# Denominators divided in token layout, sixteen-tile query sets, and gated loads in a fused linear attention and PReLU MLP

## The chip, the cores and the metric

One Trainium2 chip, one of its cores. The metric is the device time of one execution in microseconds (us); several executions of each kernel are taken and their median is used. Engines: TensorE (PE; its weight loads are PEld), VectorE (DVE), ScalarE (ACT), GpSimd (POOL), SyncE (SP), which issues most DMAs.

## The reference

q, k, v are 4 batches x 4 heads x 1088 tokens x 32, in float32. S1 and S2 are 8 x 32.

```python
def phi(x):                       # 64 features of a token
    a, b = S1 @ x, S2 @ x         # 8 and 8
    return outer(a, b).reshape(64)
kv  = sum_s phi(k)[f] * v[d]      # per batch and head, 64 x 32
z   = sum_s phi(k)                # 64
x   = (phi(q) @ kv) / (phi(q) @ z + 1e-6)     # 32 per head; four heads give 128
h   = x @ w_in                    # 4352 x 128 times 128 x 2048
g   = max(h, 0) + alpha * min(h, 0)
out = g @ w_out                   # 2048 x 128
```

## The kernel before, in words

Since g = (1 - alpha) * max(h, 0) + alpha * h, the MLP is a relu between two matmuls, plus one matmul with W = w_in diag(alpha) w_out, made once. `w_out_bf` holds w_out scaled by 1 - alpha, `w_b_f` holds w_out scaled by alpha; `winT` is w_in transposed (L319, L322); W is made at L330.

All work is written as operations (`Op`) with an engine or a choice of engines, an estimated duration, a priority and the buffers that they take and free. `schedule` lists them greedily: at each step it takes the operation that can start first, within 60 ns the one with the lowest priority number, and so fixes the order on every engine. The order is fixed when the program is built; the engines run it in order and wait for each other by semaphores. `PRIO` holds the priority bases, `UNITS` the query units, `GROUPS` the MLP's column groups. PSUM has eight banks: A0 to A3 (used by queries and keys), H0 to H2 (the first matmul's output, keys too), O (the second matmul's accumulator).

- `keys(b)`: k of a batch is transposed in blocks of 32 (VectorE, L344), multiplied by S1 and S2 (L352), transposed back to token layout (L359), and a times b gives `phi` (VectorE or POOL, L372). L404 sums phi times v over tokens on TensorE. The sum z comes for batches 0 and 1 from the same kind of products with ones, for 2 and 3 from additions of phi (L387 to L393) and one product with ones (L425). L436 transposes the result into `kz`.
- `queries(u)`: a unit of up to 1024 tokens. `qT` (L459), then features with S1 and S2 spread to 64 rows: the A part (L465) is copied out of PSUM to `a_sb` (L474), the B part (L465 again) is multiplied with it into `qp` (L480). L492 multiplies by the z part of `kz`, then by its kv part. The denominators go back to token layout (L503), are inverted (L508, L509), transposed forward again (L514) and multiplied onto the numerators (L517) into `xT`. All four A banks are held as one set through these passes.
- `mlp(g)`: for a group of columns of `xT`, 16 times: a matmul into an H bank (L533), a relu out of it to `rh` by ScalarE (L540) or VectorE (L542), a matmul into O (L546); then the one with W (L553). O is transposed to `oT` on VectorE (L558) and stored by SP.

Loads are issued by SP in the order of a list, without waits: rows (S1, S2, alpha), k0, part of q0, v0, the weights, then k, q, v of batch 1, of 2, of 3.

Of the kernel before, what the change touches and what calls it, by code (L numbers as in the profile page):

```python
# [18 lines left out]
UNITS = ((0, 256), (512, 288), (1088, 512), (2112, 512), (3136, 512), (4160, 96))  # L19
GROUPS = ((0, 512), (512, 288), (800, 288), (1088, 512), (1600, 512), (2112, 512), (2624, 512), (3136, 512),  # L20
          (3648, 512), (4160, 192))

Z_PE = (True, True, False, False)

PRIO = {"W": 5147, "w": 18782, "k": [-27032, -767, -3337, 2408], "q": [-6698, -3807, 1309, 2997, 24174, 8836]}
# [17 lines left out]
class Op:  # L43
    def __init__(self, eng, fn, prio, deps=(), takes=(), frees=(), lat=150, after=0):
# [3 lines left out]
        self.takes, self.lat, self.after = list(takes), lat, after  # L48
        for h in frees:
            h.frees.append(self)  # L50
        self.end = None


def schedule(ops, slots):


    free_at = {}
# [18 lines left out]
    while ready:  # L76
        best = None
        for o in ready:
            t0 = max([d.end + d.lat for d in o.deps] + [o.after])
# [3 lines left out]
            for h in o.takes:  # L83
                cand = sorted((slot_free(s), s) for s in h.names if s not in taken and slot_free(s) is not None)
# [19 lines left out]
        t, _, end, o, e, dur, picks = min(near, key=lambda b: (b[1], b[2]))  # L104
        o.end, free_at[e] = end, end
        for h, names in zip(o.takes, picks):
            h.got = names
            for s in names:
                holder[s] = h
# [6 lines left out]
    assert len(order) == len(ops), "operations left"  # L116
# [4 lines left out]
def kernel(  # L121
# [32 lines left out]
    rows = sb("rows", [2 * r + NC, 128])  # L154
    q_sb = sb("q_sb", [128, T])
    qT = sb("qT", [128, T])
# [6 lines left out]
    w_b_f = sb("w_b_f", [128, NC, DM])  # L163
# [4 lines left out]
    ones = sb("ones", [128, 32])  # L168
    ST = sb("ST", [128, 2 * r + NC])
    mask2 = sb("mask2", [128, 2])  # L170
    Sk = sb("Sk", [128, 2, 2 * r])
    Sa = sb("Sa", [128, r, r])
    Sb = sb("Sb", [128, r, r])
    oma = sb("oma", [128, NC])
    kz = [sb(f"kz{b}", [128, 2, 128]) for b in range(B)]

    A = psum.tile([128, 4, 512], F32, tag="A", name="A")
    bank = {f"A{i}": A[:, i] for i in range(4)}
    for i in range(3):
        bank[f"H{i}"] = psum.tile([128, 512], F32, tag=f"H{i}", name=f"H{i}")  # L180
    bank["O"] = psum.tile([128, 512], F32, tag="O", name="O")
# [13 lines left out]
    P_ab = pool("ab", 2, [128, 2, KW * 32])  # L195
    P_phi = pool("phi", 2, [128, 2, KW, 2, R])
    P_ps = pool("phs", 1, [128, 4, 2, 2, R])
    P_kv = pool("kvs", 2, [128, 2, 2, R])
    P_as = pool("a_sb", 1, [128, H, 512])
    P_qp = pool("qp", 1, [128, H, 512])  # L200
    P_dt = pool("dt", 1, [128, 2, 16, 32])
    P_rc = pool("rc", 2, [128, 2, 16])
    P_rr = pool("rr", 1, [128, 2, 512])
# [10 lines left out]
    def act(n):  # L214
        return (172 + n) / 1.2 - 10

    def dve(n):
        return (120 + n) / 0.96
# [11 lines left out]
    loads = []  # L230

    def load(name, kb, fn, after=()):
        loads.append((name, kb, fn))

    def l_rows():
        for i, x in enumerate((S1, S2)):
            dma("sync", rows[i * r:(i + 1) * r].rearrange("p (h d) -> p h d", h=H),
                dram(x, 0, [[D, r], [0, H], [1, D]]))
        dma("sync", rows[2 * r:], dram(moe_alpha, 0, [[128, NC], [1, 128]]))

    def l_k(b):
        dma("sync", k_sb[b], dram(k, b * H * S * D, [[S, 128], [1, S]]))

    def l_v(b):
        for g in range(4):
            dma("sync", v_sb[b][32 * g:32 * (g + 1)].rearrange("p h w d -> p h (w d)"),
                dram(v, b * H * S * D + K0[g] * D, [[NB * D, 32], [S * D, H], [1, KW * D]]))
# [8 lines left out]
    def l_wout(i):  # L256
        dma("sync", w_out_f[:, 8 * i:8 * (i + 1)],
            dram(moe_w_out, 8 * i * 128 * DM, [[DM, 128], [DM * 128, 8], [1, DM]]))

    plan = [("rows", 24, l_rows), ("k0", 557, lambda: l_k(0)), ("q0a", 262, lambda: l_q(0, 0, 16)),  # L260
            ("v0", 557, lambda: l_v(0)), ("wo0", 524, lambda: l_wout(0)), ("wi0", 524, lambda: l_win(0)),
            ("wi1", 524, lambda: l_win(1)), ("wo1", 524, lambda: l_wout(1)),
            ("k1", 557, lambda: l_k(1)), ("q0b", 295, lambda: l_q(0, 16, NB)), ("v1", 557, lambda: l_v(1)),
            ("q1", 557, lambda: l_q(1, 0, NB)), ("k2", 557, lambda: l_k(2)), ("v2", 557, lambda: l_v(2)),
            ("q2", 557, lambda: l_q(2, 0, NB)), ("k3", 557, lambda: l_k(3)), ("v3", 557, lambda: l_v(3)),
            ("q3", 557, lambda: l_q(3, 0, NB))]
    L = {}
    t = 700.0
    for i, (name, kb, fn) in enumerate(plan):
        t += max(kb / 0.30, 1200 if name == "rows" else 300)  # L270
        L[name] = op(("SP", 1), fn, -1000 + i, after=0, lat=0)
        L[name].lat = t + 1800


    c_ident = op(("POOL", 700), lambda: make_identity(nc, ident), -900)

    def f_masks():
        nc.vector.memset(ones, 1.0)
        nc.vector.memset(mask2, 0.0)
        for h in range(H):  # L280
            nc.vector.memset(mask2[h * D:(h + 1) * D, h % 2:h % 2 + 1], 1.0)
    c_mask = op(("DVE", 600), f_masks, -900)
    h_rows = Hold(HBANKS)
    c_rt = op(("PE", 300), lambda: nc.tensor.transpose(
        bank[h_rows.got[0]][:, :2 * r + NC], rows, ident[:2 * r + NC, :2 * r + NC]),
        -890, deps=[L["rows"], c_ident], takes=[h_rows], lat=250)
    c_st = op(("DVE", 200), lambda: nc.vector.tensor_copy(ST, bank[h_rows.got[0]][:, :2 * r + NC]),
# [3 lines left out]
    c_sa = op(("ACT", 250), lambda: nc.scalar.copy(Sa, view(ST, [[1, r], [0, r]])), -870, deps=[c_st])  # L291
    c_sb = op(("ACT", 250), lambda: nc.scalar.copy(Sb, view(ST, [[0, r], [1, r]], r)), -870, deps=[c_st])
    c_om = op(("DVE", 150), lambda: nc.vector.tensor_scalar(
        oma, ST[:, 2 * r:], -1.0, 1.0, op0=mybir.AluOpType.mult, op1=mybir.AluOpType.add), -800, deps=[c_st])


    c_win, c_wo, c_wb, c_wT = [], [], [], []
    for i in range(4):
        c_win.append(op(("ACT", 610), lambda i=i: nc.scalar.copy(
            w_in_bf[:, 512 * i:512 * (i + 1)], w_in_f[:, 512 * i:512 * (i + 1)]), PRIO["w"] + i, deps=[L[f"wi{i // 2}"]]))  # L300
    for i in range(4):
        s = slice(4 * i, 4 * i + 4)

        def scaled(e, dst, al, s=s):
            if e == "POOL":
                nc.gpsimd.tensor_mul(dst[:, s], w_out_f[:, s], view(al[:, s], [[1, 4], [0, 128]]))
            else:
                for c in range(s.start, s.stop):
                    nc.scalar.mul(dst[:, c], w_out_f[:, c], al[:, c:c + 1])
# [307 lines left out]
```

## Time and profile before

| | |
|---|---|
| median of 3 runs (lowest to highest) | 135.97 us (135.4 to 136.08) |
| profiled execution, its own time | 135.97 us |
| its span, first to last instruction | 134.2 us |
| mean granted TensorE clock | 0.983 |
| busy share of PE, DVE, ACT, POOL | 82%, 72%, 53%, 18% |
| DMA | 11.37 MB, 24271 packets |

A line of a group reads: source line, engine, operation, output and inputs with their shapes, count, then busy us, mean ns of one, and the idle time of that engine just before, with what ended it. TensorE's matmuls overlap and their ends are modelled, so its busy share overstates it; a float32 product counts as two instructions.

### The profile page before, as it was taken

Reading aid. Unit: us, or ns where it says so; the run is one execution under the profiler, and the core shown is the slowest. Engines: PE = TensorE matmul, PEld = TensorE weight load, DVE = VectorE, ACT = ScalarE, POOL = GpSimd, SP = SyncE. Lnnn points to the kernel's source line nnn. Section 1 sums busy time; section 2 is a strip of 40 time slices with the busy share of each in tenths; the row PEclk is TensorE's granted clock in tenths of the full one; section 3 lists DMA queues with packets and bytes.
Section 4 is the critical chain, followed back from the end, with each engine's and each line's share of the span. In section 5 each row is a group of like instructions: output and inputs, shape, how many; then the busy total and the mean of one; then the engine's idle time right before and its main releaser. Section 6 shows DMA issues by size and latency. Waiting matters only on the chain.

```text
span 134.2 us, 3241 instructions
## 1 busy us (share of the span) xinstructions
PE 110.1 (82%) x1315; PEld 54.4 (41%) x1315; DVE 96.4 (72%) x177; ACT 71.0 (53%) x152; POOL 24.6 (18%) x28
## 2 busy tenths in 40 slices
PE   0053899899499995988979799799998999999970
PEld 0011589565365442522724233243442444434540
DVE  0179527869999985998947775697768778598450
ACT  3105965050106944665365764497936858468640
POOL 2009740451770000992000000000000000000000
PEclk9999999999958999999999999999999999999998
DMA  1999999998000005003030001400500405014041
GB/s 31 299 255 374 358 238 334 272 286 204 26 5 7 0 3 77 0 0 49 0 48 1 0 0 24 60 0 0 78 0 12 71 0 78 0 22 68 11 67 29
DMA packets 24271, 11.37 MB, mean 85 GB/s; under 512 B 18736, under 2 KB 22848, under 8 KB 24256
## 3 DMA queue, kind: packets, MB, share of 16 engines
q1 hardware_dynamic: 24256, 11.16, 35.1%
q8 instruction: 10, 0.16, 0.6%
q14 instruction: 5, 0.04, 0.1%
HBM read 8.93 MB, written 2.23 MB: 83 GB/s over the span
## 4 chain that ended last, share of the span: by engine, by line
PE 67%; DVE 20%; DMA 4%; ACT 3%; issue 2%; SPq 1%; DVEq 0%; ACTq 0%
PE O L546 20%; PE H L533 20%; PE A L492 7%; PE A L465 6%; DVE phi L372 6%; PE H L404 5%; DVE a_sb L474 4%; DVE dt L503 4%; DMA k_sb<-in_k_dram 4%; ACT a_sb L474 3%; DVE qp L480 2%; PE H L330 2%; PE A L352 2%; DVE ab L359 2%; PE H L319 1%
## 5 line engine op out<-in xcount | busy, mean ns | idle before, releaser
L540 ACT ACTIVATE rh<-H 128x512 bf16<-128x512 f32 (+2 forms) x115 | 55.5, 532 | 26.4 <-PE H L533 24.2
L533 PE MATMUL H<-xT,w_in_bf 128*128 128x512 bf16 (+2 forms) x160 | 46.6, 348 | 1.2 <-DVE rh L542 0.6
L546 PE MATMUL O<-rh,w_out_bf 128*128 128x512 bf16 (+2 forms) x160 | 42.5, 347 | 0.0
L542 DVE TENSOR_SCALAR rh<-H 128x512 bf16<-128x512 f32 (+2 forms) x45 | 27.4, 612 | 5.8 <-PE H L533 4.8
L533 PEld LDWEIGHTS <-w_in_bf 128*128 128x128 bf16 x160 | 14.4, 97 | 22.0 <-issue 10.5
L546 PEld LDWEIGHTS <-w_out_bf 128*128 128x128 bf16 x160 | 15.5, 97 | 16.1 <-issue 2.7
L372 POOL TENSOR_TENSOR phi<-ab 128x512 f32<-128x512 f32 (+1 forms) x9 | 11.8, 1334 | 33.7 <-DVE ab L359 26.7
L492 PE MATMUL A<-qp,kz 64*32 64x512 f32 (+7 forms) x224 | 10.5, 439 | 3.3 <-DVE dt L503 2.8
L474 ACT COPY a_sb<-A 128x1024 f32<-128x1024 f32 (+2 forms) x5 | 4.3, 852 | 16.1 <-PE A L465 16.1
L480 DVE TENSOR_TENSOR qp<-a_sb,A 128x1024 f32<-128x1024 f32 (+3 forms) x12 | 10.4, 901 | 2.9 <-PE A L465 2.9
L404 PE MATMUL H<-phi,v_sb 128*32 128x64 f32 (+1 forms) x288 | 11.0, 268 | 1.2 <-issue 1.1
L558 DVE STREAM_TRANSPOSE oT<-O 128x512 f32<-128x512 f32 (+2 forms) x10 | 6.3, 628 | 5.8 <-PE O L553 5.0
L404 PEld LDWEIGHTS H<-phi,v_sb 128*32 128x32 f32 (+1 forms) x288 | 7.6, 137 | 5.6 <-issue 5.1
L474 DVE COPY a_sb<-A 128x1024 f32<-128x1024 f32 (+3 forms) x7 | 5.7, 829 | 5.7 <-ACT a_sb L474 5.7
L372 DVE TENSOR_TENSOR phi<-ab 128x640 f32<-128x640 f32 (+1 forms) x7 | 9.7, 1413 | 0.0
L465 PE MATMUL A<-qT,Sb 32*64 32x512 f32 (+3 forms) x96 | 5.7, 531 | 4.5 <-DVE a_sb L474 4.5
L503 DVE STREAM_TRANSPOSE dt<-A 128x512 f32<-128x512 f32 (+3 forms) x12 | 6.0, 538 | 2.8 <-PE A L492 2.8
L344 DVE STREAM_TRANSPOSE kT<-k_sb 128x544 f32<-128x544 f32 x8 | 5.6, 717 | 2.6 <-DMA k_sb<-in_k_dram 2.6
L352 PE MATMUL A<-kT,Sk 64*32 64x288 f32 x32 | 2.6, 549 | 5.4 <-DVE kT L344 4.0
L465 PE MATMUL A<-qT,Sa 32*64 32x512 f32 (+3 forms) x96 | 5.7, 530 | 1.1 <-DVE ab L359 1.1
L404 PE MATMUL H<-phi,ones 128*32 128x64 f32 (+1 forms) x144 | 6.4, 267 | 0.0
L514 DVE STREAM_TRANSPOSE rr<-rc 128x512 f32<-128x512 f32 (+3 forms) x12 | 5.9, 534 | 0.2
(65 smaller groups left out, 85.7 us busy)
## 6 DMA issues: line engine op xcount, KB each, us to landing
v_sb<-in_v_dram SPq DMA_DIRECT2D x16, 144.0 KB, 8.1
k_sb<-in_k_dram SPq DMA_DIRECT2D x4, 544.0 KB, 9.8
q_sb<-in_q_dram SPq DMA_DIRECT2D x3, 544.0 KB, 8.7
out_dram<-oT SPq DMA_DIRECT2D x20, 64.0 KB, 2.0
w_out_f<-in_moe_w_out_dram SPq DMA_DIRECT2D x2, 512.0 KB, 8.4
w_in_f<-in_moe_w_in_dram SPq DMA_DIRECT2D x2, 512.0 KB, 7.8
q_sb<-in_q_dram SPq DMA_DIRECT2D x1, 288.0 KB, 8.8
out_dram<-oT SPq DMA_DIRECT2D x8, 36.0 KB, 3.0
```

The costliest lines, as they stand in the source:

```text
L372: eng.tensor_mul(bufs[hph.got[0]][:, rr_, w0:w0 + m // 2].rearrange("p w h f -> p (w h) f"), view(src, [[16, m], [1, r], [0, r]], o0), vie ...
L404: nc.tensor.matmul(kb[32 * h:32 * (h + 1), (R if z else 0):(R if z else 0) + R], ones[rows_] if z else v_sb[b][rows_, h, w], p[rows_, rr_, ...
L465: nc.tensor.matmul(A[64 * c:64 * (c + 1), h, :n], S_[32 * h:32 * (h + 1)].rearrange("p i j -> p (i j)"), qT[32 * h:32 * (h + 1), col0 + c ...
L474: ca[-1].fn = lambda e, i=i: copy(e)(bufs[has.got[0]][:, 2 * i:2 * i + 2, :n], A[:, 2 * i:2 * i + 2, :n])
L480: mu.append(op(("DVE", dve(2 * n)), lambda i=i: nc.vector.tensor_mul(bufs[hqp.got[0]][:, 2 * i:2 * i + 2, :n], bufs[has.got[0]][:, 2 * i:2 ...
L492: nc.tensor.matmul(A[32 * h:32 * (h + 1), 2 * o + c, x0 - lo:x1 - lo], kz[b][64 * c:64 * (c + 1), o, 32 * h:32 * (h + 1)], bufs[hqp.got[0] ...
L503: nc.vector.transpose(bufs[hdt.got[0]][:, c, :nb].rearrange("p a b -> p (a b)"), A[:, 2 + c, :n])
L533: hm = op(("PE", n / 2.4 + 3), lambda c=c, hh=hh: nc.tensor.matmul(bank[hh.got[0]][:, :n], w_in_bf[:, c * 128:(c + 1) * 128], xT[:, col0:c ...
L540: nc.scalar.activation(bufs[hr.got[0]][:, :n], bank[hh.got[0]][:, :n], ACTF.Relu)
L542: nc.vector.tensor_scalar_max(bufs[hr.got[0]][:, :n], bank[hh.got[0]][:, :n], 0.0)
L546: nc.tensor.matmul(bank["O"][:, :n], w_out_bf[:, c], bufs[hr.got[0]][:, :n], start=state["n"] == 0, stop=state["n"] == last)
L558: ev = op(("DVE", dve(n)), lambda: nc.vector.transpose(bufs[ho.got[0]][:, :nb].rearrange("p a b -> p (a b)"), bank["O"][:, :n]), prio - 5, ...
```

## The change

Keys. k0 comes in two halves. phi is one product per head, on VectorE for batch 0 and on POOL for the others. The z sum no longer comes from phi: nine matmuls of a block of a and b with itself (`f_gram`) give the sums of a times b, VectorE picks the blocks of each head (`f_ex`), one matmul with `G` multiplies by S2 once more, and the result stands as eight more columns in `Wq[b]` beside S1 and S2. So a query's features a, b and c, with a . c the denominator, come out of one set of matmuls. `ones`, `phs`, `kz` and the products with ones go; kv is kept in `kvw`.

Queries. A unit is four runs of up to nine blocks of 32 tokens of one batch. Sixteen matmuls on 32 x 32 tiles (row of tiles h writes bank h) give a, b, c; four transposes bring them to token layout; there a is divided by a . c before a times b is made; two transposes bring the features back, and 32 matmuls on 32 x 32 tiles (row of tiles c writes bank c) give x, which is copied to `xT`. The products in between run on VectorE in the first unit and on POOL in the others.

W. w_out is not scaled by alpha; alpha is multiplied in while w_in's transposes are taken out of PSUM. The columns of w_in and rows of w_out are taken in another order (8p + c), so that w_out and alpha load in longer pieces.

Loads. k, q and v of batches 1 to 3 each wait for a memset of one element on VectorE, placed behind a step of the batch before. The small loads, and half of the last group's stores, are issued by ScalarE.

MLP. Eight groups of 512 columns and one of 256; the last two groups use the A banks for H as well.

Planner. Other prices, a cost for changes of the tile shape on TensorE, doubled durations for its early work, a model of instruction loading, warming matmuls with zeros at the start and in TensorE's waits up to 14 us, other priorities.

```diff
-UNITS = ((0, 256), (512, 288), (1088, 512), (2112, 512), (3136, 512), (4160, 96))
-GROUPS = ((0, 512), (512, 288), (800, 288), (1088, 512), ..., (4160, 192))
-Z_PE = (True, True, False, False)
+UNITS = ((0, (0, 4, 8, 12), 4, 16), (0, (16, 21, 25, 29), 5, 34), (1, (0, 9, 17, 25), 9, 34),
+         (2, (0, 9, 17, 25), 9, 34), (3, (0, 9, 17, 25), 9, 34))
+GROUPS = ((0, 512), (512, 512), ..., (3584, 512), (4096, 256))
+Q_DVE = (True, False, False, False, False)
+PHI_DVE = (True, False, False, False)
...
+    def load_batch(b, k_, q_, v_):
+        def gate(t, *deps):
+            return op(("DVE", 80), lambda: nc.vector.memset(t, 0.0), -3000, deps=deps)
+        load(f"k{b}", 2300, lambda: l_k(b), gate(k_sb[b][:1, :1], k_))
+        if b == 1:
+            load("q0b", 1300, lambda: l_q(0, 16, NB))
+        load(f"q{b}", 1900, lambda: l_q(b, 0, NB), gate(q_sb[:1, b * S:b * S + 1], q_))
+        load(f"v{b}", 2600, lambda: l_v(b), gate(v_sb[b][:1, 0, 0, :1], v_))
...
+        def f_wa(e, i=i, hb=hb):
+            x = bank[hb.got[0]].rearrange("p (c m) -> p c m", c=4)
+            if e == "DVE":
+                nc.vector.tensor_mul(winT[:, 4 * i:4 * i + 4], x, view(al[:, 4 * i:], [[1, 4], [0, 128]]))
...
+        def f_gram():
+            for w in (0, 5, 1, 6, 2, 7, 3, 8, 4):
+                rows_ = slice(0, 64) if w == 0 else slice(0, 128)
+                g = w // 5
+                x = bufs[hab.got[0]][rows_, w].rearrange("p a b -> p (a b)")
+                nc.tensor.matmul(bank[hz.got[0]][64 * g:64 * (g + 1), :64], x, x, start=w in (0, 5),
+                                 stop=w in (4, 8), skip_group_check=True)
...
+        def f_qabc():
+            for c in range(4):
+                for h in range(H):
+                    nc.tensor.matmul(bank[hA[h].got[0]][32 * c:32 * (c + 1), :n], Wq[b][32 * h:32 * (h + 1)],
+                                     bufs[hqT.got[0]][32 * h:32 * (h + 1), ...], start=True, stop=True)
...
+        ac = op(("POOL", ...) if slow else ("DVE", ...), lambda e: side(e).tensor_mul(part(2), part(2), part(0)), ...)
+        sm = op(("DVE", ...), lambda: nc.vector.reduce_sum(rd(), part(2), axis=mybir.AxisListType.X), ...)
+        ep = op(("ACT", 120) if slow else ("DVE", ...), ...)            # adds EPS
+        rc = op(("DVE", ...), lambda: nc.vector.reciprocal(rd(), rd()), ...)
+        an = op(("POOL", ...) if slow else ("DVE", ...), ...)           # a times the reciprocal
...
+            p_ = op(("POOL", ...) if slow else ("DVE", dve(4 * n)), f_p, ...)
+            mu.append(op(("DVE", ...), lambda rr_=rr_: nc.vector.transpose(bufs[hqp[rr_].got[0]][:, :4 * n], ...), ...))
...
+        def f_num():
+            for i in range(2):
+                for h in range(H):
+                    for c in range(4):
+                        nc.tensor.matmul(bank[hX[c].got[0]][32 * h:32 * (h + 1), :n],
+                                         kvw[b][32 * c:32 * (c + 1), i, 32 * h:32 * (h + 1)],
+                                         view(bufs[hqp[h // 2].got[0]][32 * c:32 * (c + 1)], [[64, nb], [1, 32]], ...),
+                                         start=i == 0, stop=i == 1, skip_group_check=True)
```

More of the change, by code (lines that the diff above doesn't have):

```diff
@@ L47, in __init__, with schedule @@
         self.deps = [d for d in deps if d is not None]
-        self.takes, self.lat, self.after = list(takes), lat, after
+        self.takes, self.lat, self.ni, self.cfg, self.glue = list(takes), lat, ni, cfg, glue
         for h in frees:
             h.frees.append(self)
-        self.end = None
-def schedule(ops, slots):
-    free_at = {}
+        self.end, self.on, self.behind, self.took = None, None, [], 0
+SWITCH, COLD, FILL = 95, 6600, 14000
+STICK = {"PE": 22100}
+def schedule(ops, slots, filler=None):
+    free_at = {"DVE": 900, "PE": 1000, "POOL": 700, "ACT": 700}
+    cfg, glued = "full", None
+    issued, have = 0, [(448, 0)]
     holder = {s: None for s in slots}
@@ L77, in schedule @@
         best = None
+        known = {}
         for o in ready:
-            t0 = max([d.end + d.lat for d in o.deps] + [o.after])
+            t0 = 0
             picks = []
@@ L115, in schedule @@
                 ready.append(u)
-    assert len(order) == len(ops), "operations left"
+    assert all(o.end is not None for o in ops), "operations left"
     return order
@@ new lines, with zeros, filler @@
+    c_mask = op(("DVE", 500), f_masks, -900, deps=[c_ident])
+    def zeros(n, name):
+        for _ in range(2 * n):
+            nc.tensor.matmul(bank[name][:, :256], warm[:, :128], warm[:, :256], start=True, stop=True)
+    def filler(n, name, each):
+        h = Hold([name])
+        return Op(("PE", each * n), lambda: zeros(n, name), 0, takes=[h], frees=[h], ni=4 * n)
+    c_warm0 = op(("DVE", 300), lambda: nc.vector.memset(warm, 0.0), -950)
+    c_warm = op(("PE", 8 * 427 + 80), lambda: zeros(8, "O"), -900, deps=[c_warm0], ni=32)
```

469 lines of the change are left out of this document (234 added, 235 removed).

## The prediction

> **What bounds the kernel now.** I read the page first, then the busy time by stage, then the chain that ended last, then the timeline of each engine. The page's own sums say that no engine is full:
>
> ```profile
> span 134.2 us, 3241 instructions
> PE 110.1 (82%) x1315; PEld 54.4 (41%) x1315; DVE 96.4 (72%) x177; ACT 71.0 (53%) x152; POOL 24.6 (18%) x28
> ```
>
> The stages say why. Columns: stretch, its length, busy us (instructions) of PE, PEld, DVE, ACT, POOL, granted clock, DMA share, GB/s.
>
> ```profile
> 0.00:20.00 20.00, 9.20 (x185) 5.43 (x189) 9.41 (x21) 9.02 (x24) 8.07 (x12) 1.00 0.92 259
> 20.00:41.00 21.00, 17.95 (x419) 12.75 (x411) 18.15 (x36) 4.47 (x10) 9.13 (x9) 0.92 0.66 182
> 48.50:80.00 31.50, 27.15 (x336) 11.88 (x335) 24.59 (x41) 18.46 (x44) 7.38 (x7) 1.00 0.13 19
> 80.00:125.50 45.50, 44.20 (x319) 18.27 (x318) 33.48 (x58) 30.43 (x54) 0.00 (x0) 1.00 0.20 30
> ```
>
> From the chain in order of time (start, us, what) and TensorE's timeline:
>
> ```profile
> 1.87 4.79 DMA k_sb<-in_k_dram
> 6.68 0.76 DVE kT L344
> 7.48 1.91 PE A L352 x16
> 9.41 0.85 DVE ab L359 x2
> 10.26 3.16 DVE phi L372 x2
> 40.92 0.37 PE H L533
> 115.56 1.73 PE O L546 x8
> 130.05 0.38 DVE oT L558
> 28.13 0.61 PE L533 MATMUL H<-xT,w_in_bf 128*128 128x512 bf16 x2
> ```
>
> Two matmuls of the MLP run at 28.13; the stream of them begins at 40.92. Before it lie 41 us in which the chain goes over loads, VectorE and half-used TensorE. In the stream a 512-column matmul takes 1.73/8 = 0.216 us. 4352 columns need 33 matmuls for every 512 (16 in, 16 out, 1 for W): 8.5 x 33 x 0.216 = 60.6 us. From the last matmul's transpose at 130.05 to the end are 4.2 us. So the span reads: 41 of start + 60.6 of MLP + the attention matmuls of the later batches + stalls + 4.2. The next rows give attention work after 41 us: features, a key set, its transposes, and (as the 48.5 to 80 row of the busy time of L404 alone) a late batch's 36 key-value products.
>
> ```profile
> 82.20 1.11 PE L465 MATMUL A<-qT,Sa 32*64 32x512 f32 x16
> 27.46 0.74 PE L465 MATMUL A<-qT,Sa 32*64 32x288 f32 x16
> 52.47 0.72 PE L352 MATMUL A<-kT,Sk 64*32 64x288 f32 x16 [1.47 <-DVE a_sb L474]
> 71.41 0.44 PE L436 MATMUL H<-ident,kvs 128*128 128x128 f32 x2
> 48.50:80.00 31.50, 1.55 (x72) 1.14 (x72) 1.00 0.13 19
> ```
>
> A 1024-column unit needs four passes such as the first row, 4.4 us. Three of them, a small unit (about 1.6, estimated by columns) and 3.5 for the last keys make 18.4 us, so the stalls are 130.05 - 40.9 - 60.6 - 18.4 = 10 us, an estimate that holds to 2 us.
>
> **The change, part by part.**
>
> *The start.* Ahead of the stream stood the keys of three batches, two query units and W. Now the first 512 tokens have a path of their own: k0 in two halves, first on SP's queue; the small rows go by ScalarE's queue. k0 was issued at 1.87 behind three small loads (the last in the first row below; SP began them 1.1 us before) and landed at 6.66, so its last half now lands about 1.1 earlier, at 5.5. Prices for what follows:
>
> ```profile
> 1.50 0.33 SPq L225 DMA_DIRECT2D rows<-in_moe_alpha_dram  x1
> L503 DVE STREAM_TRANSPOSE dt<-A 128x96 f32<-128x96 f32 x2 | 0.4, 261 | 0.0
> L503 DVE STREAM_TRANSPOSE dt<-A 128x512 f32<-128x512 f32 x6 | 3.9, 696 | 1.8 <-PE A L492 1.8
> L509 DVE RECIPROCAL rc<-rc 128x32 f32<-128x32 f32 x3 | 1.1, 353 | 0.1
> L372 DVE TENSOR_TENSOR phi<-ab x7: 782/1536/1770, 10.2 to 55.9; 128x640 f32<-128x640 f32 x5, 128x512 f32<-128x512 f32 x2
> L372 POOL TENSOR_TENSOR phi<-ab x9: 1064/1072/1869, 10.0 to 54.9; 128x512 f32<-128x512 f32 x6, 128x640 f32<-128x640 f32 x3
> L330 PE MATMUL H<-w_b_f,winT 128*128 128x128 f32 x32 | 4.2, 278 | 0.0
> L319 PE MATMUL H<-ident,w_in_f 128*128 128x128 f32 x12 | 2.3, 327 | 0.0
> ```
>
> Between the transposes' two rows a column costs 1.05 ns on 160 ns. Last half of kT 0.76: 6.2. Key features: 1.91 in this trace at 7.48, 0.72 at 52.47; the warming matmuls added ahead should bring it toward the second, I take 1.0: 7.2. Two transposes 0.85: 8.1. The new sum of keys (nine matmuls, two short VectorE operations, one matmul, a copy) has no row; between 1.2 (six handed-over operations of 0.2) and 3, I take 1.9: 10.0. Query features for 128 columns 0.5 (0.74 for 288): 10.5. Four transposes of 128 columns at 0.29: 11.7. Product, sum, epsilon, reciprocal, product, each 0.2 to 0.35: 1.4, so 13.1. Two feature products of 512 columns (782 ns for 640 when alone) and two transposes of 512: 2.8, so 15.9. On the same VectorE lie batch 0's four key products (0.7 each) and two q transposes, 3.6 us, of which about 2 fit into its waits for TensorE: 17.5. The 32 products with kv, 1.2, and the copies to xT with their waits 0.7: 19.4. I take **20 us for the start of the stream**, 18 to 24 as bounds (the key sum, and a cold clock on every TensorE step). What covers W (4.2 + 2.3 us of TensorE and four more transposes before, now without a scaled copy of w_out) is TensorE's idle time in these 20 us, between 11 and 17 above all; if that is gone it costs 7. I charge 1 us, 0 to 3. w_in is now cast with a stride, a price that no row has; ScalarE is free for it until the first relus.
>
> *Attention on TensorE after the start.* Units of 1024 tokens with four passes of eight products become one batch: 16 feature products of 288 columns and 32 of numerators, on 32x32 tiles, each row of tiles with its own bank. If sixteen run side by side, the features cost no more than 0.74 (eight side by side, 288 columns), the numerators twice that: 2.2 us for 1088 tokens, against 4.4. If only eight do, 4.4 again. I take the near row, 2.2, and keep 4.4 for the range. The denominators' products, the ones products and the z additions go. Per batch: 0.72 + new key sum 0.7 + 1.55 + 0.44 + 2.2 = 5.6; three batches 16.8, and 1.5 for the second part of batch 0: **18.3 us**, 25 with half-width sets.
>
> The Trainium skill's TensorEngine Tiling (Array Packing), Key Properties, says that a change of tiling mode drains TensorE. By it five tile shapes among bf16 matmuls cost more than the products alone; before, as many passes were interleaved, and L465's 1.11 us in the row above holds such a change, so nothing is added.
>
> *VectorE, ScalarE, POOL.* Gone: the copies of the A features, their products, both denominator transposes, the last scaling.
>
> ```profile
> L480 DVE TENSOR_TENSOR qp<-a_sb,A 128x1024 f32<-128x1024 f32 (+3 forms) x12 | 10.4, 901 | 2.9 <-PE A L465 2.9
> L474 DVE COPY a_sb<-A 128x1024 f32<-128x1024 f32 (+3 forms) x7 | 5.7, 829 | 5.7 <-ACT a_sb L474 5.7
> L503 DVE STREAM_TRANSPOSE dt<-A 128x512 f32<-128x512 f32 (+3 forms) x12 | 6.0, 538 | 2.8 <-PE A L492 2.8
> L514 DVE STREAM_TRANSPOSE rr<-rc 128x512 f32<-128x512 f32 (+3 forms) x12 | 5.9, 534 | 0.2
> L517 DVE TENSOR_TENSOR xT<-A,rr 128x512 bf16<-128x512 f32 x6 | 3.9, 676 | 0.0
> L372 DVE TENSOR_TENSOR phi<-ab 128x640 f32<-128x640 f32 (+1 forms) x7 | 9.7, 1413 | 0.0
> L540 ACT ACTIVATE rh<-H 128x512 bf16<-128x512 f32 x78 | 43.2, 599 | 17.3 <-PE H L533 16.4
> L542 DVE TENSOR_SCALAR rh<-H 128x512 bf16<-128x512 f32 x34 | 23.1, 684 | 4.6 <-PE H L533 4.2
> ```
>
> That is 28 us on VectorE and some 6 for the scaling (3.9 for six of its twelve), and about 4 on ScalarE for the five copies it took. New: twenty short transposes 8, ten long ones 11, sums and reciprocals 3.4, the first unit's products 2, twenty copies to xT 7 (by the rows' slopes). Keys lose about 9 (of the products' 9.7 some 2.9 stay, and the z additions go). The two engines go from 167 busy us to about 152. One relu each costs 0.599 and 0.684, so the pair gives one in 0.32 us where TensorE needs 0.43 for its two matmuls: TensorE stays the bound.
>
> POOL gets the products of batches 1 to 3 and of four query units: about 17,000 columns, and 2,000 of w_out. At 1072 ns for 512 that is 40 us; at 1869 for 640, 56. It has 90. Spread so, it is not the bound; the place where it is late is named below.
>
> The skill's GPSIMD Engine Reference, Engine selection, advises VectorE for elementwise products, POOL being about twice as slow. The trace agrees (1064 for 512 against 782 for 640). By that rule the products would stay on VectorE, 20 us more there, and VectorE would come close to TensorE.
>
> *Gates.* Each later batch's k, q and v wait for a one-element memset in VectorE's order. SP is in order: a load that waits holds the loads and, new here, the output stores behind it. Before, the last load was issued long ahead of the first store:
>
> ```profile
> 27.80 0.35 SPq L225 DMA_DIRECT2D q_sb<-in_q_dram  x1
> 49.41 82.81 SPq L225 DMA_DIRECT2D out_dram<-oT  x48
> k_sb<-in_k_dram SPq DMA_DIRECT2D x4, 544.0 KB, 9.8
> ```
>
> k of batch b waits only for batch b-1's key transposes; with 9.8 us to land, 0.7 + 0.7 for kT, 0.7 and 0.85 it comes round in 13 us, and a batch gives TensorE 17/8 x 7.1 + 5.6 = 20.7 us of work. Hidden; I charge nothing, and if that cover is gone the slow rival below is its price.
>
> *Stalls.* Ten before, mostly TensorE waiting for the A banks between a unit's passes (the 1.47 ahead of L352 above is one). Those passes fall from four to two and the banks are freed by short transposes. New is the wait for batch 1's queries. I take 5.5, 2 to 12.
>
> **Sum.** 20 + 60.6 + 18.3 + 1 + 5.5 + 4.2 = 109.6 us of span. The profiled execution took 135.97 us, 1.8 over its span, and is the median of the three runs: **111.4 us**. Bounds: 18 + 60.6 + 16.5 + 0 + 2 + 4 + 1.8 = 103, and 24 + 60.6 + 25 + 3 + 12 + 4.2 + 1.8 = 131 with every one at its worst.
>
> **Rivals.**
>
> *POOL late.* Before batch 1's numerators POOL must do w_out (2048 columns), batch 1's key products (2304), the second unit (1600) and batch 1's queries (2880): 8,800 columns, 18 us at 2.09 ns each, 26 at 2.92, from about 16 us on. With transposes, products and copies of 3.5 behind them they arrive at 38 or 46; TensorE asks at 20 + 14.2 + 5 = 39. Beside POOL, VectorE's own two-input product rose from 782 to 1536 ns in the row above, which stretches VectorE too. 7 us here and about 2 at each later batch: 122 us. For it: 1869 ns is seen. The skill's rule on POOL, above, points here. Against: after the first unit VectorE has few two-input products left.
>
> *Half-width sets.* The sixteen products don't run side by side, which is then a change that does not do what it says: 25 for 18.3, 118 us. Against: eight 32x64 products of 512 columns took 1.11 us, near four passes of 512 at 2.4 columns a ns, so sets do run together.
>
> *Gates and stores on one queue (slower).* If a gate stands behind VectorE's relus, its load, the stores behind that load, the three oT buffers and then bank O stop one after another. A lag of 10 us for each of three batches gives 111 + 30 = 141. It decides from (136 - 111)/3 = 8 us a batch; against 13 of 20.7 above this needs a gate 16 us late.
>
> **How the numbers follow.** About 0.5% can be told from no change. Forecast with its bounds 0.63; half-width sets 0.12; POOL late 0.17; gates 0.06; 0.02 for a loss by some sum of waits that ends at the old time. The first three are all faster: 0.92; same 0.02; slower 0.06. The range 103 to 123 holds the forecast's low bound, both middle rivals and most of its high side; what is left out is above.
>
> **What would show it.** Right: the first stream of L533's successor near 20 us; feature products of one batch below 0.8 us and numerators near 1.5; POOL near 40 us busy; relus split as before; 107 to 112 of span. Wrong: a stream that starts after 25, TensorE idle ahead of the numerators with POOL as releaser, SP waiting on VectorE while oT is full, or 16 feature products of over 1.2 us.

## The result, and the profile after

| | before | after |
|---|---|---|
| median, lowest to highest (us) | 136.03 (135.4 to 136.47), 4 runs | 111.42 (109.54 to 112.0), 4 runs |
| ratio to before, 95% interval | | 0.811 [0.800, 0.823] |
| profiled execution, span | 135.97, 134.2 | 109.54, 107.5 |
| busy share of PE, DVE, ACT, POOL | 82%, 72%, 53%, 18% | 94%, 70%, 66%, 35% |

Executions of this kernel take about 109.5 us where TensorE's mean granted clock was 1.000 and mostly 111 to 113 where it was lower; ratios are therefore compared, not single times. The prediction was 111.4 us, with a range of 103 to 123.

The page of the kernel after: span, busy time of each engine, TensorE's busy tenths and granted clock in 40 slices, and the chain's shares by engine and by line.

```profile
span 107.5 us, 3253 instructions
PE 101.0 (94%) x1309; PEld 53.9 (50%) x1309; DVE 75.1 (70%) x160; ACT 70.7 (66%) x158; POOL 37.6 (35%) x41
PE   6969999999999999999999999999999899999960
PEclk9999999999999999999999999999999999999999
PE 88%; DMA 4%; ACT 2%; DVE 1%; SPq 1%; issue 1%; ACTq 0%
PE O L615 27%; PE H L602 26%; PE A L579 6%; DMA q_sb<-in_q_dram 4%; PE H L421 4%; PE A L602 3%; PE A L527 3%; PE A L471 2%; PE A L491 2%; PE H L491 2%; PE O L355 2%; PE H L442 2%; PE O L622 2%; PE H L403 1%; PE A L442 1%; ACT rh L609 1%
```

Nearly the whole chain is TensorE now. The busy time by stage of the kernel after (columns as in the prediction; the last row is the MLP stream):

```profile
0.00:10.00 10.00, 8.02 (x70) 5.25 (x71) 5.75 (x17) 2.26 (x7) 1.09 (x11) 1.00 0.84 253
10.00:20.00 10.00, 10.00 (x231) 8.81 (x230) 9.54 (x27) 9.15 (x23) 2.08 (x2) 1.00 0.57 193
21.80:103.80 82.00, 81.20 (x966) 39.24 (x963) 58.11 (x115) 58.72 (x127) 34.38 (x28) 1.00 0.33 73
```

The chain of the kernel after, in order of time:

```profile
6.94 0.72 PE A L442 x16
9.01 0.87 PE A L471 x18
...
16.27 2.68 PE H L421 x24
18.95 1.00 PE A L579 x56
...
21.83 0.82 PE H L602 x3
...
103.76 0.45 DVE oT L627
```

L442 is the key features, L471 the new key sum, L421 is W, L579 the numerators, L602 the MLP stream's first matmul, L615 its second, L622 the one with W, L491 keys times v. The stream begins at 21.8 us instead of 40.9, and the last transpose is at 103.76 instead of 130.05. The 26.7 us of span divide so: start 19.1; attention after the start 18.4 to 17.0, so 1.4; stalls 10 to 4.3 (103.76 - 21.8 - 60.6 - 17.0), so 5.7; tail 4.2 to 3.7, so 0.5. The MLP's 60.6 is kept as predicted, so the stalls are a remainder, and not idle time: TensorE is busy for 81.2 of the 82 us. In the chain the MLP's own lines (L615, L602, L622) have 58.6% of the span before rounding, 63.0 us; by that count the MLP's matmuls took 2.4 us more than 60.6, and 1.9 us are left for everything between.

TensorE's timeline of the kernel after answers the two widths that were in doubt:

```profile
26.60 0.77 PE L527 MATMUL A<-qT,Wq 32*32 32x288 f32 x32
44.39 1.60 PE L579 MATMUL A<-qp,kvw 32*32 32x288 f32 x64
```

Sixteen feature products of 288 columns (two instructions each) take 0.77 us, 32 numerators 1.60, both without a wait ahead. Half-width sets are excluded.

### The profile page after: what moved, and what is told of

It is laid out like the page before. It is cut to its first block, busy times and chain, and to the rows that moved or that the text cites. A ratio compares the mean times of both kernels' runs of the same rounds, so it can differ in the third digit from the quotient of the medians.

```text
span 107.5 us, 3253 instructions
## 1 busy us (share of the span) xinstructions
PE 101.0 (94%) x1309; PEld 53.9 (50%) x1309; DVE 75.1 (70%) x160; ACT 70.7 (66%) x158; POOL 37.6 (35%) x41
## 4 chain that ended last, share of the span: by engine, by line
PE 88%; DMA 4%; ACT 2%; DVE 1%; SPq 1%; issue 1%; ACTq 0%
PE O L615 27%; PE H L602 26%; PE A L579 6%; DMA q_sb<-in_q_dram 4%; PE H L421 4%; PE A L602 3%; PE A L527 3%; PE A L471 2%; PE A L491 2%; PE H L491 2%; PE O L355 2%; PE H L442 2%; PE O L622 2%; PE H L403 1%; PE A L442 1%; ACT rh L609 1%
## 5 line engine op out<-in xcount | busy, mean ns | idle before, releaser
L609 ACT ACTIVATE rh<-H 128x512 bf16<-128x512 f32 (+1 forms) x91 | 48.2, 593 | 10.5 <-PE H L602 10.2
L615 PE MATMUL O<-rh,w_out_bf 128*128 128x512 bf16 (+1 forms) x144 | 40.4, 367 | 0.0
L602 PE MATMUL H<-xT,w_in_bf 128*128 128x512 bf16 (+1 forms) x124 | 38.7, 374 | 0.6 <-ACT rh L609 0.6
L611 DVE TENSOR_SCALAR rh<-H 128x512 bf16<-128x512 f32 (+1 forms) x33 | 21.3, 652 | 9.7 <-PE H L602 8.1
L615 PEld LDWEIGHTS <-w_out_bf 128*128 128x128 bf16 x144 | 13.9, 97 | 17.6 <-issue 5.7
L602 PEld LDWEIGHTS <-w_in_bf 128*128 128x128 bf16 x144 | 13.3, 98 | 15.9 <-issue 3.3
L457 POOL TENSOR_TENSOR phi<-ab 128x576 f32<-128x576 f32 x12 | 13.8, 1177 | 13.1 <-DVE ab L449 13.1
L562 POOL TENSOR_TENSOR qf<-qa 128x1152 f32<-128x1152 f32 (+1 forms) x8 | 15.5, 1952 | 0.2
L566 DVE STREAM_TRANSPOSE qp<-qf 128x1152 f32<-128x1152 f32 (+2 forms) x10 | 11.2, 1124 | 0.7 <-POOL qf L562 0.7
L609 ACT ACTIVATE rh<-A 128x512 bf16<-128x512 f32 (+1 forms) x16 | 7.1, 505 | 3.2 <-PE A L602 2.9
L355 PE MATMUL O<-warm 128*128 128x256 bf16 x42 | 7.5, 342 | 1.1 <-DVE warm L360 1.1
L579 PE MATMUL A<-qp,kvw 32*32 32x288 f32 (+2 forms) x320 | 7.0, 364 | 0.0
L579 PEld LDWEIGHTS A<-qp,kvw 32*32 32x32 f32 x320 | 3.9, 103 | 2.5 <-issue 1.3
```

What stands on the lines that cost most here:

```text
L355: nc.tensor.matmul(bank[name][:, :256], warm[:, :128], warm[:, :256], start=True, stop=True)
L457: eng.tensor_mul(bufs[hph.got[0]][:, rr_, :, h2].rearrange("p w (i j) -> p w i j", i=r), view(src, [[64, KW], [1, r], [0, r]], 32 * rr_ + ...
L562: side(e).tensor_mul(bufs[hqf[rr_].got[0]][:, :4 * n].rearrange("p (m i j) -> p m i j", i=r, j=r), view(src, [[32, 2 * nb], [1, r], [0, r] ...
L566: mu.append(op(("DVE", dve(4 * n) + 40), lambda rr_=rr_: nc.vector.transpose(bufs[hqp[rr_].got[0]][:, :4 * n], bufs[hqf[rr_].got[0]][:, :4 ...
L579: nc.tensor.matmul(bank[hX[c].got[0]][32 * h:32 * (h + 1), :n], kvw[b][32 * c:32 * (c + 1), i, 32 * h:32 * (h + 1)], view(bufs[hqp[h // 2] ...
L602: hm = op(("PE", n / 2.4 + 3), lambda c=c, hh=hh: nc.tensor.matmul(bank[hh.got[0]][:, :n], w_in_bf[:, c * 128:(c + 1) * 128], xT[:, col0:c ...
```

## The experiments

**The kernel after, again**, with no edit, for the spread.

> The changed kernel again, unchanged, as the yardstick for the runs beside it. Its profiled execution took 109.54 us at a mean granted clock of 1.000; three other executions took 111.1 to 112.0 at 0.984. Theory one (the clock loses one stretch early in some executions): the times fall in two clusters some 2 us apart, and the clock tells which. Theory two (plain scatter of the loads): times spread evenly between 109.5 and 112 with no tie to the clock.

Median 111.75 of 6 (109.45 to 112.89), ratio 0.808 [0.801, 0.814]. Times with their mean clock: 109.45 at 1.000, 110.15 at 0.997, 111.63 and 111.86 at 0.984, 112.89 at 0.964; one, 112.75 at 0.994, doesn't fit. So the spread goes mostly with the clock. Where it goes is seen in the profiled execution of this run (111.63 us): the clock of the page, TensorE's timeline, and the first two stages.

```profile
PEclk9985999999999999999999999999999999999999
```
```profile
7.31 1.10 PE L442 MATMUL A<-kT,Sk 64*32 64x288 f32 x16 [1.83 <-DVE Sk L368]
...
8.61 2.34 PE L355 MATMUL O<-warm 128*128 128x256 bf16 x10
```
```profile
0.00:10.00 10.00, 7.04 (x47) 4.28 (x48) 4.95 (x16) 2.00 (x6) 1.09 (x11) 0.88 0.83 238
10.00:20.00 10.00, 9.94 (x182) 8.46 (x181) 8.52 (x22) 7.28 (x18) 2.48 (x2) 0.95 0.55 200
```

TensorE stood 1.83 us ahead of the key features and then ran slower: they took 1.10 us instead of 0.72, and ten zero matmuls 2.34 us where 1.25 stands in the faster profile. The loss of 0.12 x 10 + 0.05 x 10 = 1.7 us is most of the 2.1 between the two profiled times. In the faster one the wait at this place was 0.92 us and the clock stayed. The profiles of the runs below, which came from several chips, agree. With the zero matmuls in place, a wait ahead of the key features of 0.80 us (gates open) or none (set-up steps first) went with a granted clock of 1.00 in the first 20 us. Waits of 1.74 to 2.47 us went with 0.79 to 0.97 in each of the first two stages in six profiles (this one, all products on VectorE, the key sum twice, POOL twice, alpha, no division). In a seventh (POOL twice, planned anew: 1.90 us) the granted clock reads 1.00, and yet the key features took 1.21 us: the granted clock doesn't show every slow start.

**The small set-up steps first.** Those waits ended with `Sk`, which VectorE made late: ahead of it in VectorE's order stood two q transposes that wait for q's load.

```profile
5.83 0.77 DVE L518 STREAM_TRANSPOSE qT<-q_sb 128x256 f32<-128x256 f32 x2 [0.51 <-DMA q_sb<-in_q_dram]
6.52 0.14 DVE L366 COPY ST<-H 128x16 f32<-128x16 f32 x1
6.69 0.19 DVE L368 TENSOR_TENSOR Sk<-ST,mask 128x32 f32<-128x32 f32 x1
```

The edit moves the first unit's q transposes behind the steps made of S1 and S2 in the planned order. These five VectorE instructions then change places, and nothing else:

```diff
-DVE: qT, qT, ST, Sk, Y, ...
+DVE: ST, Sk, Y, qT, qT, ...
```

> On VectorE the copy of S1 and S2 out of PSUM and the two products made of it come ahead of the first unit's q transposes; nothing else moves. In the changed kernel they stand behind these transposes, which wait for q (first q transpose at 5.83 us, key features at 6.94, TensorE idle 0.92 us before them; in the repeat 6.20, 7.31 and 1.83 us, and there the clock falls to half from 8 to 12 us). Theory one (VectorE's order sets the key features and the idle time sets the clock): key features at about 5.5, the MLP's stream 1 us earlier, and fewer executions at 0.984: 108.5 to 109.5 in most. Theory two (the start is set elsewhere, by W on TensorE ahead of the first numerators): no more than 0.3 us.

Median 109.71 of 6 (109.36 to 110.64), ratio 0.806 [0.802, 0.811]. TensorE's timeline, and from the chain the steps that now bound the start:

```profile
5.99 0.72 PE L442 MATMUL A<-kT,Sk 64*32 64x288 f32 x16
...
18.32 1.07 PE L579 MATMUL A<-qp,kvw 32*32 32x128 f32 x64
...
21.64 0.66 PE L602 MATMUL H<-xT,w_in_bf 128*128 128x512 bf16 x2 [0.16 <-DVE ab L449]
```
```profile
4.13 5.86 DMA w_in_f<-in_moe_w_in_dram
11.44 1.35 DVE winT L411 x2
...
18.15 5.60 DMA q_sb<-in_q_dram
```

The key features come 0.95 us earlier and without a wait, but the numerators only 0.56 (18.88 to 18.32): next in the chain are w_in's load and the VectorE step that takes w_in's transposes out of PSUM. The stream's first matmul comes only 0.13 earlier (21.77 to 21.64), and behind it the chain goes over batch 1's q load, which its gate lets go at 18.1 us. The best time is unchanged (109.4), so theory two was right on the amount; all six executions had a clock of at least 0.992, so theory one was right on the clock. This is the best version tried: its best equals the kernel after's, its spread is 1.3 us where that had 3.4. The interval of the ratio overlaps the other's, so the gain shown is in the median over executions, 111.4 to 111.75 against 109.71. It ran on another chip than the repeat; the kernel before had mean clocks of 0.968 to 0.999 on this one and 0.975 to 1.000 on the other, so the chip is an unlikely cause, but the unchanged kernel was not run on this one.

**No warming.** The zero matmuls are left out, the order is kept.

```diff
-        for _ in range(2 * n):
+        for _ in range(0):
```

> The zero matmuls that warm TensorE at the start and fill its waits are left out (nothing of the result is); the order stays. Theory one (they keep the clock up): key features at 1.8 instead of 0.72, key sum, W and the key-value products slower, the stream 2 to 4 us later and the time with it. Theory two (the real work raises the clock soon enough): 1 us or less.

Median 111.18 of 4, ratio 0.817 [0.812, 0.821], some 1.2 us over the kernel after by the ratios, whose intervals overlap: between the theories. TensorE's timeline of this run:

```profile
7.63 1.22 PE L442 MATMUL A<-kT,Sk 64*32 64x288 f32 x16 [3.06 <-DVE Sk L368]
...
9.86 1.52 PE L471 MATMUL A<-ab 64*64 64x64 f32 x18 [0.61 <-DVE ab L449]
```

Key features 1.22 and key sum 1.52 instead of 0.72 and 0.94; from 15 us on the products have their later durations. The mean granted clock of these four executions is 0.992 to 1.000, so it shows nothing of this slow start. What warming saves, a single early wait can lose again.

**Gates open.** The memset of each gate writes a spare element, so the loads wait for nothing; every order is the same.

```diff
-            return op(("DVE", 80), lambda: nc.vector.memset(t, 0.0), -3000, deps=deps)
+            return op(("DVE", 80), lambda: nc.vector.memset(spare, 0.0), -3000, deps=deps)
```

> The gates' memsets write a spare element, so the loads of batches 1 to 3 no longer wait for VectorE; the order of every engine stays. Theory one (hidden cover): the later batches' data come early enough either way, so the time stays within 1 us of the changed kernel. Theory two (the gates keep SP free for the stores or the DMA engines free for others): without them something later is late, 2 to 5 us more. Theory three (the gates cost, since SP's queue holds): 1 to 3 us less.

Median 115.0 of 6, ratio 0.837 [0.830, 0.844]: (0.837 - 0.8076) x 136 = 4.0 us slower. Theories one (the data come early enough either way) and three (the gates cost) fell; the size is theory two's. TensorE's timeline shows where:

```profile
26.24 0.61 PE L602 MATMUL H<-xT,w_in_bf 128*128 128x512 bf16 x1 [3.32 <-issue]
26.78 1.52 PE L471 MATMUL A<-ab 64*64 64x64 f32 x18
```

For 3.32 us TensorE waits for nothing that the profile shows as a release, and then runs slower for some us (18 instructions of the key sum in 1.52 for 0.94). The DMA queues of this run, from 22 to 23 and from 23 to 24 us (packets, MB, share of 16 engines), and of the kernel after from 0 to 20, name what came late:

```profile
q1 hardware_dynamic: 118, 0.34, 97.7%
```
```profile
q1 hardware_dynamic: 155, 0.21, 105.0%
q8 instruction: 1, 0.02, 9.0%
```
```profile
q1 hardware_dynamic: 1892, 4.41, 68.8%
...
q8 instruction: 2, 0.03, 0.8%
```

In the kernel after, two packets of instructions come in the first 20 us. Without gates only one does, the loads hold the DMA engines full, and the second comes between 23 and 24, during the stand. So the gates' gain is shown; that the late packet is what TensorE stood for is read from their order in time only. Against it stands the run without warming: its gates were in place, and there too one packet came before 20 us and the second between 23 and 24, with q1 at 105.1%, and TensorE didn't stand. What differs is how long the queue was full: from 12 us at least to 25 here, from 22 to 25 there. The next run tried it by another way.

**Gates open and no warming**, both edits together, so that other instructions stand at the place.

> The loads without gates, as in the run that took 115.0 us with TensorE standing from 22.9 to 26.2 us for nothing that the profile names, and the 42 zero matmuls left out as well (111.2 us with gates). Theory one (that stand is TensorE waiting for its next block of instructions, which lies in line with the loads: the block boundary is a count of instructions, so with 84 fewer it comes some 4 us later in the work, when the loads are done): the stand shrinks below 1.5 us, 111 to 113 us. Theory two (it waits for loaded data or a bank): the stand stays at the same matmul, 114 to 117 us.

Median 114.07 of 4, ratio 0.829 [0.821, 0.837]. TensorE's timeline:

```profile
22.58 0.83 PE L579 MATMUL A<-qp,kvw 32*32 32x128 f32 x36 [2.14 <-issue]
```

The stand is 2.14 us and lies inside one set of numerators, between its 28th and 29th instruction, where no operand can be missing; the second instruction packet came between 24 and 26 us by the same queue rows, after it had ended. That it moved to another place speaks against a cause in the work at the old one. But it moved earlier in the work, where fewer instructions ahead should have let a fixed place in the program come later, and the packet is late for it. That opening the gates of this kernel makes TensorE stand is shown twice; which fetch it stands for, and where, stays open. Nor must ungated loads do so: the kernel before has them, with its queue about full from 12 to 32 us, and TensorE's one wait there without a releaser is 1.08 us at 34.4.

**All products on VectorE.**

```diff
-Q_DVE = (True, False, False, False, False)
-PHI_DVE = (True, False, False, False)
+Q_DVE = (True, True, True, True, True)
+PHI_DVE = (True, True, True, True)
...
-        if not slow:
+        if u == 0:
```

> All products of phi and of the query features on VectorE, none on POOL; the planner orders anew. VectorE gets about 17,000 columns, 21 us at 782 ns for 640. Theory one (TensorE is the bound with room on VectorE, 75 of 107 us busy): VectorE rises to about 93 us and the time by 2 to 5 us, from relus that wait. Theory two (POOL's products are the long pole, by their latency): the time falls by 1 to 3 us. Theory three (VectorE becomes the bound): 118 us or more.

Median 120.01 of 6, ratio 0.871 [0.864, 0.878]: 8.7 us slower (8.0 between the best executions). VectorE is busy 89.8 us of 120.4, not full over the whole; but by stage, and in TensorE's timeline just behind:

```profile
40.00:50.00 10.00, 8.13 (x64) 3.48 (x62) 9.69 (x16) 7.05 (x16) 0.00 (x0) 1.00 0.08 13
```
```profile
50.15 0.72 PE L579 MATMUL A<-qp,kvw 32*32 32x288 f32 x16 [2.02 <-DVE qp L566]
51.41 2.21 PE L579 MATMUL A<-qp,kvw 32*32 32x288 f32 x48 [0.54 <-DVE qp L566]
```

At batch 1 VectorE has both the relus and the products to do, is 9.7 of 10 busy, and TensorE waits for the query's products. Theory three's size and theory one's mechanism, at one place.

**POOL's key products twice**, once with the order kept and once planned anew with the doubled duration.

```diff
-                eng.tensor_mul(bufs[hph.got[0]][...
+                for _ in range(1 if e == "DVE" else 2): eng.tensor_mul(bufs[hph.got[0]][...
```
```diff
-            e = {"DVE": dve(KW * R)} if PHI_DVE[b] else {"POOL": 50 + KW * R * 2}
+            e = {"DVE": dve(KW * R)} if PHI_DVE[b] else {"POOL": 2 * (50 + KW * R * 2)}
```

> POOL makes each key product of batches 1 to 3 twice (same result, same order): 13.8 us more on POOL, 37.6 to 51, of which 4.6 per batch ahead of that batch's query products. Theory one (POOL has slack, as in the sum): batches 2 and 3 hidden, at batch 1 a delay of 4.6 against little slack: 1 to 5 us. Theory two (POOL late, the rival): every batch delays the stream, 9 us or more. Theory three (no effect): under 1 us.

> The key products on POOL twice, as in the run before it that took 127.7 us, but here the planner knows their doubled duration and orders anew. Theory one (a fixed order shows every lateness in full; TensorE has other matmuls to do): most of the 17 us comes back, 111 to 118 us. Theory two (POOL's chain per batch is the bound whatever the order): 122 us or more.

With the order kept: ratio 0.934 [0.928, 0.940], 17 us slower for 14 more on POOL, which is then busy for only 42% of the span. Planned anew: 0.923 [0.917, 0.929], so the planner gets some 1.5 us of 17 back, if anything (the intervals just overlap). The chain's shares by engine with the order kept, its waits, and TensorE's timeline planned anew:

```profile
PE 57%; POOL 27%; DVE 5%; DMA 4%; issue 3%; SPq 1%; ACT 0%; ACTq 0%
```
```profile
DVE qp L566 <- POOL qf L562: 9.1, 4, 4.9
PE H L602 <- DVE rh L611: 7.4, 3, 3.7
```
```profile
55.47 2.28 PE L491 MATMUL H<-phi,v_sb 64*32 64x64 f32 x66 [3.19 <-POOL phi L457]
```

VectorE waits in order for POOL's products, its relus stand behind that wait, and TensorE waits for the relus (7.4 us). Theory two held: POOL has no slack to speak of. Part of the 17 us can be clock: TensorE's mean granted clock was 0.93 to 0.94 in all executions of both runs, and with the order kept 0.87 from 75 to 90 us, after a wait of 3.68 us at 69. How much it is was not measured apart.

**The key sum twice.**

```diff
-            for w in (0, 5, 1, 6, 2, 7, 3, 8, 4):
+            for w in (0, 5, 1, 6, 2, 7, 3, 8, 4) * 2:
```

> The nine matmuls of the key sum are issued twice (same result, same order otherwise), 0.87 us more of TensorE for each of four batches, three of them after the MLP's stream has begun. Theory one (TensorE bound throughout): 2.6 us more for the three, and up to 0.9 for the first, which lies on the way to the stream: 2.6 to 3.5 us. Theory two (relus or POOL bound, TensorE merely shown busy by modelled ends): 0 to 1 us.

Ratio 0.833 [0.827, 0.840], 3.5 us slower (3.9 between the best executions). Four batches by 0.87 us (L471 in the chain) are 3.5: within the intervals, what TensorE is given more, the kernel takes longer, and no stall swallows it.

**No division.** The five steps from a . c to a times the reciprocal are left out.

> The denominators are left out: no product a . c, no sum, no reciprocal, no scaling of a (the output is then the numerators' through the MLP); every order stays. It frees 5.0 us on POOL, about 4.6 on VectorE, and 1.7 on the first unit's way. Theory one (the division is hidden: the first numerators wait for W until 18.9 us in any case, later units have slack): within 0.5 us. Theory two (it lies on the path): 1.5 us less or more.

Median 110.54 of 4 (108.22 to 110.71). That is 0.9 to 1.2 us under the two medians of the kernel after, and the best is 1.2 under its best (109.45): between the theories. TensorE's timeline of this run, where the clock was reduced early as above:

```profile
18.26 2.84 PE L421 MATMUL H<-w_out_f,winT 128*128 128x128 f32 x24
21.03 1.07 PE L579 MATMUL A<-qp,kvw 32*32 32x128 f32 x64
```

The first numerators stand right behind W's last matmul, as they do with the division. Its 1.4 us of steps in the start are hidden behind W, so theory one holds there. That leaves the later units for the 1.2 us, which no view here shows.

**Alpha on a second copy of w_out**, as before, planned anew.

```diff
-                nc.vector.tensor_mul(winT[:, 4 * i:4 * i + 4], x, view(al[:, 4 * i:], [[1, 4], [0, 128]]))
+            copy(e)(winT[:, 4 * i:4 * i + 4], x)
...
+            nc.gpsimd.tensor_mul(w_b_f[:, s], w_out_f[:, s], view(al[:, s], [[1, 4], [0, 128]]))
```

> W's alpha multiplied onto a second copy of w_out again (on POOL or ScalarE, as in the kernel before), w_in's transposes copied plainly; the planner orders anew. It adds four scalings of 512 columns, 1.04 us each on POOL or 1.2 on ScalarE, ahead of W's matmuls. Theory one (W lies on the path to the stream, TensorE doing it from 14.9 to 18.9 us just ahead of the first numerators): 1 to 3 us more. Theory two (W is covered): within 1 us.

Ratio 0.820 [0.814, 0.827], 1.7 us slower (the intervals just touch), POOL 41.2 us busy instead of 37.6. That is theory one's size, but not its wait. In TensorE's timeline W's last matmul ends at 21.19, and the first numerators wait for VectorE:

```profile
22.14 1.07 PE L585 MATMUL A<-qp,kvw 32*32 32x128 f32 x64 [0.95 <-DVE kvw L510]
```

This profile has an early wait of 1.82 us and its slow start as well, so the cause of the 1.7 us is not shown.

**Before, with its first MLP group put first.** In the kernel before, only this group's priority is changed.

```diff
-        mlp(g, c0, n, 1000 * g, ...
+        mlp(g, c0, n, 1000 * g - (60000 if g == 0 else 0), ...
```

> The kernel before with one change: the first MLP group has the lowest priority number, so its matmuls come as soon as its 512 columns are there (28 us instead of 41). Theory one (what counts is TensorE's work and idle time, not where the stream begins): the moved work comes back behind it, and only idle time of 28 to 41 is won: 131 to 137 us. Theory two (an early stream is itself the gain): about 136 - 12 = 124 us.

Ratio 0.982 [0.976, 0.987], 2.5 us faster. Its chain, and the stage behind:

```profile
30.66 0.75 PE H L533 x3
```
```profile
41.00:60.00 19.00, 14.92 (x233) 7.38 (x223) 16.45 (x29) 8.08 (x20) 9.45 (x10) 0.91 0.06 10
```

The same stage of the kernel before:

```profile
41.00:60.00 19.00, 17.00 (x140) 7.76 (x144) 17.25 (x29) 12.99 (x31) 6.14 (x5) 1.00 0.10 15
```

The stream begins 10 us earlier, and most of that is lost again from 41 us on. TensorE then issues 233 instructions where the kernel before has 140, the attention work that was put off, and it is idle for 4.1 us instead of 2.0, at a clock of 0.91. Theory one held: beginning early is worth little while the work ahead of the later batches stays; the change took work out there.

## Why the prediction was right

**Term by term.** Start of the stream, W beside it included, 21 predicted (20 and 1), 21.8 measured. Of this W holds about 0.4: the first numerators' operand was ready at 18.45 (17.16 + 1.29 on VectorE), they began at 18.88, after W. Attention after the start 18.3, 17.0. MLP 60.6 and stalls 5.5: together 66.1 against 64.9; by the chain's shares it was 63.0 and 1.9, so the MLP was sized too small and the stalls too large. Tail 4.2, 3.7. Outside the span 1.8, 2.0. The errors are of both signs, at most 2.4 us but for the stalls' 3.6, so the sum is better than its terms: 111.4 against a median of 111.42, and 109.6 of span against 107.5 at full clock. What the median holds beyond the undisturbed 109.5 is the slow start, which no term named. That the number was met to 0.02 us is luck: the sum was 2 us too long, and the slow start of most executions filled it up.

**The start.** The key features took 0.72 with a wait of 0.92 (predicted 1.0, finishing at 7.2; they ended at 7.7). The step that failed is small: the prediction has no term for the copies of S1 and S2, and they stood behind two transposes waiting for q. The reordered run removes that and shows the next bound, w_in's load. The other loss was in the first unit: its first two-input product took 0.57 us and ended at 14.76, just after POOL's scaling of w_out (14.61); the next one took 0.29. With the set-up steps first the same product took 0.29 while POOL was scaling, and the epsilon addition 0.65 instead of 0.17, which ended at 14.94 with POOL's end at 14.91. So one step of the unit was held until POOL ended, and not every step beside POOL is.

```profile
14.19 0.57 DVE L548 TENSOR_TENSOR qa<-qa 128x128 f32<-128x128 f32 x1
...
15.61 0.29 DVE L555 TENSOR_TENSOR qa<-qa,rd 128x128 f32<-128x128 f32 x1
```

**TensorE stays the bound.** Right: 81.2 of 82 us busy in the stream, and the doubled key sum costs its own time within the intervals. VectorE and ScalarE together are 145.8 us busy (75.1 + 70.7; predicted 152). The sets run sixteen side by side, as the 0.77 us above shows.

**POOL.** Its work was sized well (37.6 us against 40), and it did not come late. But the step "it has 90. Spread so, it is not the bound" was mis-sized: a busy share is not slack. Each batch's products stand between two VectorE steps, and 14 us more cost 17 with the order kept and 15.7 planned anew. That is the mechanism of the rival "POOL late". It did not decide here, but it was near: batch 1's features, made by POOL, were all transposed at 43.8 us (the line below), and TensorE began their numerators at 44.4, not at the 39 that the rival had it ask.

```profile
42.40 1.37 DVE L566 STREAM_TRANSPOSE qp<-qf 128x1152 f32<-128x1152 f32 x1
```

On the rule weighed there (the Trainium skill, GPSIMD Engine Reference, Engine selection): the groups of the kernel after agree that POOL is the slower engine:

```profile
L457 POOL TENSOR_TENSOR phi<-ab 128x576 f32<-128x576 f32 x12 | 13.8, 1177 | 13.1 <-DVE ab L449 13.1
L457 DVE TENSOR_TENSOR phi<-ab 128x576 f32<-128x576 f32 x4 | 2.8, 739 | 0.0
```

But keeping the products on VectorE costs 8.7 us, so the measurement decides against the advice for this kernel.

**Gates.** "Hidden; I charge nothing" held as to the cost: the gated loads cost nothing that the result shows, and the gates' rival (141 us) did not occur. The cover is thin at batch 1: with the set-up steps first, its gated q load is in the chain. But the question was put from one side only: what a late load costs. The open gates show the other side, 4 us that the gates save in this kernel.

**Division, alpha.** The first unit's division was charged 1.4 us on the path; measured, it nearly ties with W: the numerators began right behind W, about 0.4 us after their operand was ready. So W adds 0.4 to the path with the division, and the division alone adds nothing to the path with W. The scaled copy of w_out that the change leaves out was given no price; the run that puts it back, planned anew, took about 1.7 us more.

## What to carry to other kernels

Take work out ahead of the bounding engine rather than reorder it: an earlier start alone gave 2.5 us, the whole change, which takes work out as well, 24.6. Test an engine's slack by doubling its work, since 35% busy meant next to none here; and put set-up steps that depend on nothing late ahead of steps that wait for a load on the same in-order engine. Try holding back loads that nobody needs yet: it was worth 4 us here.

## What the runs showed of the hardware

- TensorE stood for 3.3 us, and in another run 2.1, with nothing to wait for in the program, while ungated loads kept the main DMA queue at about 100% (94.6% to 106.9% in each microsecond from 19 to 24). Three such microseconds with gates (94.6% to 105.1%) had no such stand.
- After some 5 us of zero matmuls, waits of TensorE of 1.74 to 2.47 us were followed by slower products in seven profiles, in six of them with a reduced granted clock (0.79 to 0.97 in each of the first two 10 us); waits of 0.80 and 0.92 us and none at all were not. Where the limit lies between 0.92 and 1.74 is open.
- A VectorE step beside POOL's scaling of w_out could be held until POOL ended: a product of 128 columns took 0.57 us instead of 0.29, an addition of 16 columns 0.65 instead of 0.17. In the second of these runs the same product took 0.29 beside POOL.
- Sixteen float32 products of 288 columns on 32 x 32 tiles take 0.77 us, as eight on 32 x 64 tiles took 0.74 before.
